# A transformer block in split fp32 on one core: the odd blocks' squares pass DRAM unrounded and are split on arrival, row stores go to ScalarE's queue, and some loads are issued at other places

## The chip, the cores and the metric

The kernel runs on one core of a Trainium2 chip. The metric is the device time of one execution in microseconds. The kernel before took 1139.48 us, the median of three runs (1138.54 to 1140.03).

## The reference, cut to what matters

```python
# S = 2048 rows, D = 576, 32 heads of Dh = 18, F = 4608, all fp32
def _A_ref(x, wqkv, wo):
    q, k, v = heads(x @ wqkv)
    W, dil = 8, 2                                     # each row sees itself and 7 rows, 2 apart
    idx = pos[:, None] - (arange(W) * dil)[None, :]
    logits = einsum("bhsd,bhswd->bhsw", q, k[idx]) * Dh ** -0.5
    attn = softmax(where(idx >= 0, logits, -1e9))
    return einsum("bhsw,bhswd->bhsd", attn, v[idx]) @ wo

def _B_ref(x, w1, b1, w2, b2):
    r = relu(x @ w1 + b1)
    return (r * r) @ w2 + b2

xn = layernorm(x)
out = x + _A_ref(xn, wqkv, wo) + _B_ref(xn, w1, b1, w2, b2)
```

## The kernel before, in words

**Split operands.** Every fp32 operand of a product is split in two: a rounded part `hi`, copied by ScalarE, and the rest `lo`, subtracted by VectorE (the helper `tt`, L94). A product is three matmuls: hi by hi, hi by lo, lo by hi.

**Blocks and stages.** The 2048 rows are four blocks b of 512 (TB), taken in two pairs s: (0, 1) and (2, 3). The stages follow each other on TensorE:

- the opening: x of block 0 is normalized row by row and turned, and the first of four head groups g gets its Q, K and V;
- `q0()` (L1072): the 28 other quarter-block rows of Q, K, V of blocks 0 and 1, 14 matmuls each;
- `phase_a(0)` (L634): the FFN of blocks 0 and 1 in 18 pairs p of 128-wide slices of F. `ffn_pair` (L505) forms both blocks' products x W1 together (L525, L529). Block 0's squares are multiplied with W2 at once (L494); block 1's go to DRAM. About 17.7 us a pair;
- block 0's attention output times wo, in five chunks c (`o_hi`, `o_lo`, `o_ops`);
- `phase_b0` (L759): block 1's squares come back from DRAM and are multiplied with W2, tile by tile (n = 0 to 35); between them the Q, K, V rows of blocks 2 and 3; then block 1 times wo;
- `phase_a(1)`, block 2 times wo, `phase_b1` (L835) and the tail: the same for blocks 2 and 3.

**The odd block's squares.** In `ffn_pair`, r0 and r1 are the two blocks' relu sums, in buffers `r4` (four of them, also used for u, for parts of Wqkv, for a part of the regrouped attention output and for o). In `finish_pair` (L545) ScalarE makes `h1`'s rounded square of r1 (L536) and the full square (L540), VectorE subtracts (L94, `h<-r,h`), and SP stores hi and lo, 1024 KB, in `hscr`. `load_h` (L755) brings both back into one of three `h` buffers, three pairs ahead.

**Q, K, V rows.** `qkv_out` (L294): ScalarE copies a row's sums into one of four slots j of the one buffer `st` (L295), and every second row three DMAs on SP store two slots in DRAM. A slot is written again four rows later, so the copy waits for the landing of that store. Five TensorE banks hold rows that are not yet copied. `split_wq` splits the next head group's weights on ScalarE (L261) and VectorE.

**Attention.** For each block and group, `attention(b, g)` (L343) is 18 pieces on VectorE; `side(k)` hands out k of them at places fixed in the code. Its q, k and v come from DRAM by `fetch()` in the order of `offer()`; they are issued on `lane[0]`, which is SP at first and POOL from row 6 of `q0` on. At the end of an attention eight stores on POOL (L382) write its output, and `release()` lets the next loads go. POOL works its queue in order: the stores, the q, k and v loads, and `regroup` (L683, L689), which reads a block's whole attention output (part 0 into `st`, part 1 into an `r4`). `o_hi` (L693) transposes that on VectorE (L700).

**Weights.** `load_w2` (L452, L457) keeps three raw tiles `w2r` and three split ones `w2s`; `w2_hi` and `w2_lo` split two tiles ahead. `load_w1` (L428) brings W1 of a pair in two 640 KB loads. Both are issued on SP, in program order with everything else there.

Of the kernel before, what the change touches and what calls it, by code (L numbers as in the profile page):

```python
# [8 lines left out]
F32 = mybir.dt.float32  # L9
# [7 lines left out]
P = 128  # L17
S, D, F = 2048, 576, 4608
H, DH, W, DIL = 32, 18, 8, 2
TB = 512  # L20
# [25 lines left out]
def block_kernel(ctx: ExitStack, tc: tile.TileContext, x, xt, wqkv, wo, w1, b1, w2, b2, out):  # L46
# [30 lines left out]
    b1t = const.tile([P, NF], F32, name="b1t")  # L77
    b2t = const.tile([P, 64], F32, name="b2t")[:, :NC]

    scr = {k: [dram.tile([PAD + S, CG], F32, name=f"{k}scr{g}") for g in range(G)] for k in "kvq"}  # L80
    OPART = ((0, OA), (OA, CG))
    oscr = {(b, k): dram.tile([P, NJ * G, z - a], F32, name=f"o{b}{k}") for b in range(NB) for k, (a, z) in enumerate(OPART)}
    mrscr = {b: dram.tile([2 * NJ, P], F32, name=f"mr{b}") for b in range(1, NB)}
    hscr = [[dram.tile([P, 4 * TB], F32, name=f"h{s}{p}") for p in range(NP)] for s in range(2)]

    def flat(t, off, parts, n):
        a = t[0:1, 0:1]
# [206 lines left out]
    def qkv_out(b, g, j, p):  # L294
        nc.scalar.activation(stage[0][:, j], p[:, :QW], AF.Copy)  # L295
        if j % 2:
            for i, k in enumerate("kvq"):
                nc.sync.dma_start(scr[k][g][PAD + b * TB:PAD + (b + 1) * TB].rearrange("(p j) c -> p j c", j=NJ)[:, j - 1:j + 1],
                                  stage[0][:, j - 1:j + 1, i * CG:(i + 1) * CG])

    def qkv_row(b, g, j, i):
        p = bank(i)
# [6 lines left out]
        a = t[:, j:j + 1, 0:1]  # L309
        return bass.AP(tensor=a.tensor, offset=a.offset, ap=[a.ap[0], [DIL * CG, W], *dims])  # L310

    loads, landed, queue, free, lane = [], {}, [], [0], [nc.sync]

    def fetch():
        while free[0] and loads:
            free[0] -= 1
            kind, b, g = loads.pop(0)
            if kind == "x":
                load_rows(b)
                landed["x", b] = True  # L320
                continue
            t = landed[kind, b, g] = sb.tile([P, NE, CG], F32, name="kv", bufs=3)
            if kind == "k":
                q = landed["q", b, g] = sb.tile([P, NJ, CG], F32, name="q", bufs=2)
                lane[0].dma_start(q.rearrange("p j c -> p (j c)"),
                                  flat(scr["q"][g], (PAD + b * TB) * CG, [NJ * CG, P], NJ * CG))
            lane[0].dma_start(t.rearrange("p e c -> p (e c)"),
                              flat(scr[kind][g], (PAD + b * TB - HALO) * CG, [NJ * CG, P], NE * CG))
# [176 lines left out]
    def ffn_pair(s, p, work, first=False):  # L505
# [38 lines left out]

        def finish_pair():  # L545
            r0, r1, h0 = prev.pop("r")
            h1 = square_hi(r1)
            square_lo(r0, h0)
            square(r1)
            yield  # L550
            square_lo(r1, h1)
            nc.sync.dma_start(hscr[s][p], h1.rearrange("p k f t -> p (k f t)").bitcast(F32))
            yield

        before = prev.pop("finish", None)
# [7 lines left out]
        if not last:  # L563
            combine_w1(n + 1)
        if not first:
            side(1 + p % 2, False)
        work(0)
        product(bb, T2, ss(2))
        w2_hi()
# [64 lines left out]
    def phase_a(s, filler):  # L634
        b = 2 * s
        ffn_pair(s, 0, filler, first=True)
        open_y(b)
        for p in range(1, NP):
            h, ops = hs.pop(s * NP + p - 1), []

            def work(i):
                if i in (0, 2):
                    ops.extend(tile_products(b, 2 * p - 2 + i // 2, h))
                add(b, ops[7 * i:7 * i + 7])

            if p == NP - 1:
                complete(b)
                regroup(b, 0)
                residual(b)
                if s == 0:  # L650
                    load_xt(2)
                    load_mb(2)
            ffn_pair(s, p, work)
        h, end = hs.pop(s * NP + NP - 1), prev.pop("finish")
        load_h(s, 0)
        next(end)
        regroup(b, 1)
        o_hi(b, 0), o_hi(b, 1)
        o_lo(b, 0), o_lo(b, 1)
        add(b, tile_products(b, NF - 2, h))  # L660
        w2_hi()
        w2_lo()
        next(end)
        load_h(s, 1)
        residual_left(b)
        o_hi(b, 2), o_hi(b, 3)
        o_lo(b, 2), o_lo(b, 3)
        add(b, tile_products(b, NF - 1, h))
        w2_hi()
        w2_lo()  # L670
        o_hi(b, 4)
        o_lo(b, 4)
        for c in range(NC):
            w2_hi()
            add(b, o_ops(b, c), range(NC) if c == NC - 1 else ())
            w2_lo()
            if c == 1:
                load_h(s, 2)
        finish(b)

    ob = {}
# [72 lines left out]

    def load_h(s, p):  # L755
        t = hs[s, p] = mt.tile([P, 2, 2, TB], F32R, name="h", bufs=3)
        nc.sync.dma_start(t.rearrange("p k f t -> p (k f t)").bitcast(F32), hscr[s][p])

    def phase_b0():  # L759
        b, r = 1, 0  # L760
        todo = [(2 + i, g, j) for g in range(G) for i in range(2) for j in range(NJ)]
        split_up.clear()
        open_stage()
        load_xt(3)
        load_wq(0)
        pieces = [normalize(2), once(load_mb, 3), split_wq(0, "S", lambda: load_wq(1)), normalize(3)]
        open_y(b)
        for n in range(NF):
            w2_hi()
            add(b, tile_products(b, n, hs[0, n // 2]))  # L770
            w2_lo()
            if n % 2 and n // 2 + 3 < NP:
                load_h(0, n // 2 + 3)
            run(pieces, 2 if n < 9 else 1)
            while r < 32 and 32 * (n - 6) > 22 * r:
                bb, g, j = todo[r]
                while bb not in normed or g not in split_up:
                    run(pieces, 1)
                qkv_row(bb, g, j, 2 + r % 3)
                r += 1  # L780
                if r == 2:
                    pieces.append(split_wq(1, "w1s", lambda: load_wq(2)))
                if r == 8:
                    pieces.append(split_wq(2, "S", lambda: load_wq(3)))
                if r == 16:
                    pieces.append(split_wq(3, "w1s"))
                if r == 24:
                    pieces.append(sums(1))
                if j == NJ - 1 and bb == 2:
                    offer(2, g)  # L790
                run(pieces, 2)
            if n == 28:
                run_all(pieces)
                last_sum(1)
                complete(1)
                load_w1(NP)
                load_w1(NP + 1)
                regroup(b, 0)
                regroup(b, 1)
                for g in range(G):  # L800
                    offer(3, g)
            if n == 33:
                residual(b)
                combine_w1(NP)
            if n in (33, 34):
                c = 2 * (n - 33)
                o_hi(b, c), o_hi(b, c + 1)
                o_lo(b, c), o_lo(b, c + 1)
        o_hi(b, 4)
        o_lo(b, 4)  # L810
        residual_left(b)
        for c in range(3):
            w2_hi()
            add(b, o_ops(b, c))
            w2_lo()
            if c == 1:
                w1_hi(NP, 0)
                w1_lo(NP, 0)

        def filler(i):  # L820
            if i < 2:
                add(b, o_ops(b, 3 + i), range(NC) if i else ())
            if i == 0:
                w1_hi(NP, 1)
                w1_lo(NP, 1)
            if i == 1:
                finish(b)

        return filler
# [5 lines left out]
    def phase_b1():  # L835
        b = 3
        open_y(b)
        for n in range(NF - 2):
            w2_hi()
            add(b, tile_products(b, n, hs[1, n // 2]))  # L840
            w2_lo()
            if n % 2 and n // 2 + 3 < NP:
                load_h(1, n // 2 + 3)
            if b not in xr and (n == 22 or not queue and current[0] is None):
                complete(b)
                regroup(b, 0)
                regroup(b, 1)
                residual(b)
                residual_left(b)
            if n in range(27, 27 + NC):  # L850
                o_hi(b, n - 27)
                o_lo(b, n - 27)
            side(2)
        for c in range(NC):
            w2_hi()
            add(b, o_ops(b, c), (NC - 2,) if c == NC - 1 else ())
# [215 lines left out]
    def q0():  # L1072
        todo = [(b, g, j) for b, g in ((0, 1), (0, 3), (0, 2), (1, 3), (1, 2), (1, 1), (1, 0)) for j in range(NJ)]
        pieces = [statistics(1), split_wq(3, "S")]

        held = []

        def row(r):
            b, g, j = todo[r]
# [3 lines left out]
            if j == NJ - 1:  # L1083
# [2 lines left out]
                    if not b and g > 1:  # L1086
                        offer({3: 2, 2: 3}[g])

                if r < 2:
                    held.append(go)  # L1090
                else:
                    go()

        for r in range(len(todo) - 2):
            row(r)
            if r == 1:
                run(pieces, 1)
                turn_mr(1, 7)
                load_mb(1)
            if r == 2:  # L1100
                run_all(pieces)
                load_wq(2)
                offer(0, 0)
                for late in held:
                    late()
                held.clear()
                pieces += [normalize(1)]
            if r == 6:
                lane[0] = nc.gpsimd
                load_w1(0)  # L1110
                pieces.insert(0, split_wq(2, "h", lambda: load_wq(0)))
            if r == 11:
                run_all(pieces)
            if r == 15:
# [91 lines left out]
```

## Time and profile before

| | before |
|---|---|
| median of three runs | 1139.48 us |
| profiled execution | 1139.25 us |
| its span | 1137.5 us |
| granted TensorE clock, mean | 0.998 |
| DMA, mean over the span | 224 GB/s |

In the views quoted below, a row of a timeline is start and length in us, engine, line, operation, output and inputs, count, and in brackets the idle time ahead of it with what ended it. A row of a group is count, busy us, mean ns, and the idle us ahead. A row of the waits is the total idle us, the number of waits, and the longest. A row of a window is its length, then the busy us (and instructions) of TensorE, its weight loads, VectorE, ScalarE and POOL, then the granted clock, the DMA engines' share and GB/s. A row of DMA issues is count, KB each and the median us from issue to landing. A row of the chain is start, length and what the time was spent on.

### The profile page before, as it was taken

The numbers are of one execution on the slowest core, as the hardware profiler recorded it, in microseconds if no ns is written. First come the engines' busy times: TensorE is split into PE (matmuls) and PEld (weight loads), VectorE is DVE, ScalarE is ACT, GpSimd is POOL, SyncE is SP. The second block draws the span as 40 slices with busy tenths as digits, with TensorE's granted clock in tenths as the row PEclk, the third lists the DMA queues.
The fourth block names the chain that finished last, engine by engine and source line by source line (L and its number), as shares of the span: only waits on it lengthen the run. The fifth ranks groups of instructions, "written<-read, shape, count | busy, mean of one in ns | idle before, by whom it ended". The sixth has DMA issues, their size and how long they took to land.

```text
span 1137.5 us, 13818 instructions
## 1 busy us (share of the span) xinstructions
PE 1117.7 (98%) x5014; PEld 937.1 (82%) x5014; DVE 912.6 (80%) x1202; ACT 575.1 (51%) x801; POOL 115.1 (10%) x219
## 2 busy tenths in 40 slices
PE   8899999999999999999999899999999999999998
PEld 6799788888888887889998777888888888887787
DVE  7696999899988966888777779789897978789453
ACT  5334767666666663422222256766667666422131
POOL 4001001020200100022101001001020100101100
PEclk9999999999999999999999999999999999999999
DMA  7857544576575679887785944645464562887982
GB/s 278 293 178 221 183 167 165 194 188 218 185 204 189 212 270 327 331 306 241 252 275 168 346 160 158 234 139 191 173 234 161 181 240 100 290 305 256 343 296 88
DMA packets 89477, 254.26 MB, mean 224 GB/s; under 512 B 12472, under 2 KB 40896, under 8 KB 74816
## 3 DMA queue, kind: packets, MB, share of 16 engines
q1 hardware_dynamic: 78576, 200.86, 50.9%
q0 software_dynamic: 10544, 52.14, 14.0%
q8 instruction: 39, 0.64, 0.2%
q10 hardware_dynamic: 288, 0.37, 0.1%
q14 instruction: 30, 0.25, 0.1%
HBM read 191.90 MB, written 61.43 MB: 223 GB/s over the span
## 4 chain that ended last, share of the span: by engine, by line
PE 83%; DVE 7%; DMA 5%; issue 2%; ACT 1%; SPq 1%; POOL 1%; ACTq 0%; DVEq 0%; POOLq 0%
PE p L494 35%; PE p L525 29%; PE p L305 13%; PE p L529 5%; DMA w2r<-in_w 2%; DVE w2s L94 2%; DVE pr L94 1%; PE p L989 1%; DMA h<-h 1%; DMA qscr<-st 1%; DVE w1s L94 1%; DVE lg L354 1%; DMA q<-qscr 1%; DVE w1r L94 0%; DVE h L94 0%
## 5 line engine op out<-in xcount | busy, mean ns | idle before, releaser
L494 PE MATMUL p<-h,w2s 128*128 128x512 f32 x2010 | 486.4, 390 | 3.4 <-DMA h<-h 1.4
L494 PEld LDWEIGHTS p<-h,w2s 128*128 128x128 f32 x2010 | 376.2, 188 | 86.4 <-ACT w2s L467 2.7
L525 PE MATMUL p<-X,w1s 128*128 128x512 f32 x864 | 219.5, 389 | 1.6 <-DVE r L94 1.6
L525 PEld LDWEIGHTS p<-X,w1s 128*128 128x128 f32 x864 | 162.0, 188 | 36.0 <-DVE r L94 2.4
L94 DVE TENSOR_TENSOR w2s<-w2r,w2s 128x576 fp32r<-128x576 f32 x164 | 123.4, 755 | 84.0 <-ACT w2s L467 83.5
L467 ACT ACTIVATE w2s<-w2r 128x640 fp32r<-128x640 f32 x164 | 119.6, 733 | 119.1 <-DMA w2r<-in_w 63.6
L525 PE MATMUL p<-S,w1s 128*128 128x512 f32 x648 | 164.6, 389 | 0.0
L525 PEld LDWEIGHTS p<-S,w1s 128*128 128x128 f32 x648 | 121.5, 188 | 25.5 <-DVE r L94 0.3
L382 POOL DMA_DIRECT2D o<-q x128 | 69.4, 607 | 620.2 <-DVE q L94 618.2
L94 DVE TENSOR_TENSOR h<-r,h 128x1024 fp32r<-128x1024 f32 (+2 forms) x78 | 93.1, 1198 | 42.5 <-ACT r L540 35.4
L295 ACT ACTIVATE st<-p 128x432 f32<-128x432 f32 x64 | 33.6, 529 | 145.1 <-PE p L305 93.9
L94 DVE TENSOR_TENSOR w1s<-w1r,w1s 128x1024 fp32r<-128x1024 f32 x72 | 88.1, 1223 | 23.4 <-ACT w1s L440 23.3
L532 ACT ACTIVATE r<-r,b1t 128x512 f32<-128x512 f32 x72 | 52.0, 722 | 108.4 <-DVE r L94 108.4
L94 DVE TENSOR_TENSOR pr<-q,kv 128x1152 f32<-128x1152 f32 x64 | 86.8, 1356 | 1.3
L94 DVE TENSOR_TENSOR pr<-lg,kv 128x1152 f32<-128x1152 f32 x64 | 86.7, 1355 | 1.2
L354 DVE TENSOR_REDUCE lg<-pr 128x64 f32<-128x1152 f32 x64 | 86.4, 1350 | 0.9
L94 DVE TENSOR_TENSOR pr<-pr 128x576 f32<-128x576 f32 (+1 forms) x128 | 77.7, 607 | 3.5
L440 ACT ACTIVATE w1s<-w1r 128x1024 fp32r<-128x1024 f32 x72 | 75.7, 1052 | 4.0 <-PE p L494 4.0
L536 ACT ACTIVATE h<-r 128x1024 fp32r<-128x1024 f32 x72 | 76.0, 1056 | 1.1
L540 ACT ACTIVATE r<-r 128x1024 f32<-128x1024 f32 x72 | 76.0, 1055 | 1.2
L529 PE MATMUL p<-x,w1s 128*128 128x512 f32 x216 | 66.5, 389 | 0.0
L494 PE MATMUL p<-w1s,w2s 128*128 128x512 f32 x260 | 61.0, 391 | 3.5 <-ACT w2s L467 3.3
(135 smaller groups left out, 1043.8 us busy)
## 6 DMA issues: line engine op xcount, KB each, us to landing
h<-h SPq DMA_DIRECT2D x72, 1024.0 KB, 5.5
w2r<-in_w SPq DMA_DIRECT2D x144, 320.0 KB, 4.7
w1r<-in_w SPq DMA_DIRECT2D x36, 640.0 KB, 4.8
kv<-vscr POOLq DMA_DIRECT2D x15, 1296.0 KB, 8.0
kv<-kscr POOLq DMA_DIRECT2D x14, 1296.0 KB, 8.2
r<-in_wqkv SPq DMA_DIRECT2D x16, 432.0 KB, 5.9
w2r<-in_wo SPq DMA_DIRECT2D x20, 320.0 KB, 4.8
w1r<-in_xt SPq DMA_DIRECT2D x6, 1024.0 KB, 7.5
```

The source lines that it names most:

```text
L94: return nc.vector.tensor_tensor(out=out, in0=a, in1=b, op=op)
L305: nc.tensor.matmul(p[:, :QW], l, r, start=k == 0, stop=k == len(mm) - 1)
L354: nc.vector.tensor_reduce(out=lg[:, j * HG:(j + 1) * HG].rearrange("p a w -> p w a"), in_=pr.rearrange("p w (a d) -> p w a d", d=DH), axis ...
L382: nc.gpsimd.dma_start(rows[:, i], q[i * L:(i + 1) * L, :, a:z])
L440: nc.scalar.activation(w1s[n, k][:, 0], raw1[n][:, 4 * k:4 * k + 4], AF.Copy)
L467: nc.scalar.activation(w2s[stream[i]][:, :DE], raw2[i], AF.Copy)
L494: nc.tensor.matmul(yp[b][c], v, a, start=c not in yb[b], stop=c in last and c not in [o[0] for o in ops[i + 1:]], skip_group_check=True)
L525: nc.tensor.matmul(to, l, r, start=start and i == 0, stop=i == len(mm) - 1, skip_group_check=True)
L529: nc.tensor.matmul(to, weight(LEFT, k, f), v, start=False, stop=k == 1, skip_group_check=True)
L532: nc.scalar.activation(to, a, AF.Relu, bias=b1t[:, f:f + 1])
L536: nc.scalar.activation(h[:, 0], r, AF.Square)
L540: nc.scalar.activation(r, r, AF.Square)
```

## The change

Six parts:

1. `hscr` is half as large. `finish_pair` squares r1 in place (L540) and stores that, unrounded; the square `h1` and its subtraction are gone. `load_h` loads 512 KB into the `lo` half of the tile; the new `h_hi` copies it rounded into the `hi` half on ScalarE, and `h_lo` subtracts in place on VectorE. They are called for pair 0 in the wo part of `phase_a`, and for the next pair at every second tile of `phase_b0` and `phase_b1`.
2. The Q, K, V rows are stored by ScalarE's queue; the three scratches of a group are parts of one DRAM tile.
3. In `q0`, block 1's statistics are turned and loaded (`turn_mr`, `load_mb`) after row 2 rather than row 1; the first attentions' loads are offered after row 6, on POOL, rather than after row 2, on SP; `load_w1(0)` moves from row 6 to row 10.
4. In phase A, `side()` at the start of a pair gives 2 + p % 2 pieces in pair pass 0 (it was 1 + p % 2) and 1 + p % 2 in pass 1 (as before); for p = 1 it gives 1 (it was 2).
5. In `phase_b0`, `load_w1(NP)` moves from tile 28 to tile 20; at tile 28 the regroups are issued ahead of the attention's next loads, and `load_w1(NP + 1)` behind those.
6. In `phase_b1`, `side(2)` becomes `side(1 + n % 2)`.

```diff
-    scr = {k: [dram.tile([PAD + S, CG], F32, name=f"{k}scr{g}") for g in range(G)] for k in "kvq"}
+    kvq = [dram.tile([3, PAD + S, CG], F32, name=f"kvq{g}") for g in range(G)]
+    scr = {k: [kvq[g][i] for g in range(G)] for i, k in enumerate("kvq")}
...
-    hscr = [[dram.tile([P, 4 * TB], F32, name=f"h{s}{p}") for p in range(NP)] for s in range(2)]
+    hscr = [[dram.tile([P, 2 * TB], F32, name=f"h{s}{p}") for p in range(NP)] for s in range(2)]
...
-                nc.sync.dma_start(scr[k][g][PAD + b * TB:PAD + (b + 1) * TB].rearrange("(p j) c -> p j c", j=NJ)[:, j - 1:j + 1],
-                                  stage[0][:, j - 1:j + 1, i * CG:(i + 1) * CG])
+                nc.scalar.dma_start(scr[k][g][PAD + b * TB:PAD + (b + 1) * TB].rearrange("(p j) c -> p j c", j=NJ)[:, j - 1:j + 1],
+                                    stage[0][:, j - 1:j + 1, i * CG:(i + 1) * CG])
...
     def fetch():
-        while free[0] and loads:
+        while free[0] and loads and not held[0]:
...
         def finish_pair():
             r0, r1, h0 = prev.pop("r")
-            h1 = square_hi(r1)
             square_lo(r0, h0)
             square(r1)
             yield
-            square_lo(r1, h1)
-            nc.sync.dma_start(hscr[s][p], h1.rearrange("p k f t -> p (k f t)").bitcast(F32))
+            nc.sync.dma_start(hscr[s][p], r1.rearrange("p f t -> p (f t)"))
             yield
...
         if not first:
-            side(1 + p % 2, False)
+            side(1 if p == 1 else (2 if s == 0 else 1) + p % 2, False)
...
         for c in range(NC):
             w2_hi()
+            if c == 2:
+                h_hi(s, 0)
             add(b, o_ops(b, c), range(NC) if c == NC - 1 else ())
             w2_lo()
             if c == 1:
                 load_h(s, 2)
+            if c == 2:
+                h_lo(s, 0)
...
-        nc.sync.dma_start(t.rearrange("p k f t -> p (k f t)").bitcast(F32), hscr[s][p])
+        nc.sync.dma_start(t[:, 1].rearrange("p f t -> p (f t)").bitcast(F32), hscr[s][p])
+
+    def h_hi(s, p):
+        if p < NP:
+            t = hs[s, p]
+            nc.scalar.activation(t[:, 0], t[:, 1].bitcast(F32), AF.Copy)
+
+    def h_lo(s, p):
+        if p < NP:
+            t = hs[s, p]
+            tt(t[:, 1], t[:, 1].bitcast(F32), t[:, 0].bitcast(F32), ALU.subtract)
...
         for n in range(NF):
             w2_hi()
+            if n % 2 == 0:
+                h_hi(0, n // 2 + 1)
             add(b, tile_products(b, n, hs[0, n // 2]))
             w2_lo()
+            if n % 2 == 0:
+                h_lo(0, n // 2 + 1)
...
+            if n == 20:
+                load_w1(NP)
             if n == 28:
                 run_all(pieces)
                 last_sum(1)
+                held[0] = True
                 complete(1)
-                load_w1(NP)
-                load_w1(NP + 1)
                 regroup(b, 0)
                 regroup(b, 1)
+                held[0] = False
+                fetch()
+                load_w1(NP + 1)
...
-            side(2)
+            side(1 + n % 2)
...
-                if r < 2:
-                    held.append(go)
+                if r < 6:
+                    waiting.append(go)
...
-            if r == 1:
-                run(pieces, 1)
+            if r == 2:
                 turn_mr(1, 7)
                 load_mb(1)
-            if r == 2:
                 run_all(pieces)
                 load_wq(2)
-                offer(0, 0)
-                for late in held:
-                    late()
-                held.clear()
                 pieces += [normalize(1)]
             if r == 6:
                 lane[0] = nc.gpsimd
+                offer(0, 0)
+                for late in waiting:
+                    late()
+                waiting.clear()
+                pieces.insert(0, split_wq(2, "h", lambda: load_wq(0)))
+            if r == 10:
                 load_w1(0)
-                pieces.insert(0, split_wq(2, "h", lambda: load_wq(0)))
```

More of the change, by code (lines that the diff above doesn't have):

```diff
@@ L310, in shifted @@
         return bass.AP(tensor=a.tensor, offset=a.offset, ap=[a.ap[0], [DIL * CG, W], *dims])
-    loads, landed, queue, free, lane = [], {}, [], [0], [nc.sync]
+    loads, landed, queue, free, lane, held = [], {}, [], [0], [nc.sync], [False]
     def fetch():
-        while free[0] and loads:
+        while free[0] and loads and not held[0]:
             free[0] -= 1
@@ L839, in phase_b1 @@
             w2_hi()
+            if n % 2 == 0:
+                h_hi(1, n // 2 + 1)
             add(b, tile_products(b, n, hs[1, n // 2]))
             w2_lo()
+            if n % 2 == 0:
+                h_lo(1, n // 2 + 1)
             if n % 2 and n // 2 + 3 < NP:
@@ L1074, in q0 @@
         pieces = [statistics(1), split_wq(3, "S")]
-        held = []
+        waiting = []
         def row(r):
```

## The prediction

> **What bounds the kernel now.** I read three views: the busy shares and the chain of waits on the page, then what TensorE's idle time waited for, then timelines around each wait.
>
> ```profile
> PE 1117.7 (98%) x5014; PEld 937.1 (82%) x5014; DVE 912.6 (80%) x1202; ACT 575.1 (51%) x801; POOL 115.1 (10%) x219
> ...
> PE 83%; DVE 7%; DMA 5%; issue 2%; ACT 1%; SPq 1%; POOL 1%; ACTq 0%; DVEq 0%; POOLq 0%
> ```
> ```profile
> PE p L494 <- ACT w2s L467: 4.7, 5, 2.2
> PE p L305 <- ACT h L261: 4.3, 1, 4.3
> ...
> PE p L525 <- DVE r L94: 1.6, 2, 0.9
> PE p L494 <- DMA h<-h: 1.4, 1, 1.4
> PE p L163 <- POOL mr L130: 1.0, 1, 1.0
> ```
>
> TensorE is busy 98% of the span. No matmul is added or removed, so a gain can come only out of its idle time, and behind the start-up this list holds nearly all of it: 4.7 + 4.3 + 1.6 + 1.4 + 1.0 = 13.0 us in ten places. (Some cost a little more, since the clock falls behind them.) A loss has no such ceiling: whatever makes TensorE wait in a new place is added whole. So I go through the ten waits, and then look for an eleventh.
>
> **The opening.** The longest single wait:
>
> ```profile
> 44.39 0.55 PE L305 MATMUL p<-S,x 128*128 128x432 f32 x2
> 49.28 4.29 PE L305 MATMUL p<-h,X 128*128 128x432 f32 x12 [4.34 <-ACT h L261]
> ...
> 53.80 2.50 PE L305 MATMUL p<-h,X 128*128 128x432 f32 x12
> ...
> 56.54 2.50 PE L305 MATMUL p<-h,X 128*128 128x432 f32 x12
> ```
> ```profile
> 28.22 0.29 PE p L163
> ...
> 39.34 0.37 SPq L298
> ...
> 40.27 7.14 DMA qscr<-st
> ```
>
> The 12 matmuls behind the gap take 4.29 us, where the same 12 take 2.50 later: a gap of this length costs 1.8 us beyond itself. The chain says why it opens. ScalarE must copy the next row's sums into `st`, whose slot is free only when the stores issued from 39.34 have landed, 7.14 us after the last issue; the split of the weights (L261) stands behind that copy. The change acts on it from both sides.
> - For: the 1.0 us wait of L163 goes, since the statistics are turned a row later. The q, k and v loads that crowd the stores leave SP for POOL, where nothing is ahead of them, so they start and end earlier, and the stores could land in 2 to 4 us rather than 7.
> - Against: a row takes 56.54 - 53.80 = 2.74 us, so L163 moves from 28.22 to about 28.22 - 1.0 + 2.74 = 30.0, and with it the normalized block, on which ScalarE waits ahead of its copies. ScalarE now issues the stores itself, three per pair of rows at about 0.37 us and a little more each: 1.2 us at the least.
>
> With landings as long as now, TensorE resumes about 1.8 + 1.2 = 3.0 us later than at 49.28; with landings 3 to 5 us shorter, between then and 2 us earlier. I take 0.3 us gained, between -3 and +2. Later in this stage the same stores delay nothing as long as TensorE's five banks hold the rows that ScalarE has not copied.
>
> The Trainium skill (DMA: Bandwidth & Descriptors, Issuing engines are not separate DMA queues) speaks against part of this: transfers started by any engine share the same 16 DMA engines, and a second issuing engine saves only its issue time. By that rule alone the landings would stay at 7.14 us, the opening would lose 3.0 us, and the forecast would be 3.3 us later; that loads start earlier is not covered by it, and no run here shows it yet.
>
> **Phase A's steady part.** Two of the ten waits are in pairs 1 and 19, for VectorE's sum `r` (1.6 us in all). Each pair loses the subtraction `h<-r,h` of the odd block; in phase A(0) one more piece of attention is put in its place; and pairs 1 and 19 lose a piece besides.
>
> ```profile
> L94 DVE TENSOR_TENSOR h<-r,h 128x1024 fp32r<-128x1024 f32 x32 | 39.1, 1222 | 15.0 <-ACT r L540 15.0
> L94 DVE TENSOR_TENSOR pr<-q,kv 128x1152 f32<-128x1152 f32 x18 | 24.4, 1356 | 0.3
> ```
> ```profile
> 130.00:418.00 288.00, 287.36 (x1268) 237.59 (x1268) 253.51 (x344) 188.10 (x247) 30.06 (x55) 1.00 0.63 207
> ```
>
> Pairs 1 and 19 become 1.22 + 1.36 = 2.6 us lighter, more than the longest wait there (0.9): both waits go, 1.6 us gained. In the other pairs of A(0) the exchange is -1.22 + 1.36 = +0.14 us, hidden behind VectorE's idle 288 - 254 = 34 us over 16 pairs, about 2 us a pair. I take nothing; without that cover it would be 16 x 0.14 = 2.2 us. ScalarE's 36 fewer squares only make it freer here.
>
> **The end of phase A(0): the eleventh wait.** Some 16 more pieces in A(0) are nearly an attention (18 pieces), so attentions end at other places. In the order of the changed kernel's instructions, attention (1,2) ends in pair 17: its last `q` on VectorE stands behind the pair's sum r0. Behind it on POOL's queue come its eight stores, the next q load (which waits until all eight have landed), a k load, and only then the regroup r<-o of block 0, which TensorE needs for the wo products. In before this regroup was long through:
>
> ```profile
> 416.12 0.69 DVE L94 TENSOR_TENSOR r<-p,r 128x512 f32<-128x512 f32 x1 [0.95 <-PE p L529]
> 416.73 1.35 DVE L94 TENSOR_TENSOR pr<-lg,kv 128x1152 f32<-128x1152 f32 x1
> ...
> 426.43 0.67 DVE L700 STREAM_TRANSPOSE r<-r 128x512 f32<-128x512 f32 x1
> ```
> ```profile
> 425.99 14.90 PE L494 MATMUL p<-w1s,w2s 128*128 128x512 f32 x65
> ```
> ```profile
> DMA  9999999999996779100000189999999999896799
> ...
> r<-o POOLq DMA_DIRECT2D x1, 384.0 KB, 6.8
> ```
>
> (The first line is the DMA engines' busy share, in tenths, in 40 slices of 1.125 us from 400 on; the second has the microseconds from issue to landing.)
>
> Exactly this sequence is in the trace already, at the end of phase A(1), where it has room:
>
> ```profile
> 963.33 1.25 DVE L94 TENSOR_TENSOR pr<-pr 128x576 f32<-128x576 f32 x2
> 964.61 0.31 DVE L94 TENSOR_TENSOR q<-pr 128x144 f32<-128x144 f32 x1
> ```
> ```profile
> 965.21 1.64 POOL L382 DMA_DIRECT2D o<-q  x3 [42.67 <-DVE q L94]
> 967.23 2.69 POOL L382 DMA_DIRECT2D o<-q  x5 [0.38 <-issue]
> 975.04 0.56 POOL L325 DMA_DIRECT2D q<-qscr  x1 [5.12 <-DMA o<-q]
> 975.59 0.56 POOL L327 DMA_DIRECT2D kv<-kscr  x1
> 976.12 0.56 POOL L689 DMA_DIRECT2D r<-o  x1
> ```
> ```profile
> r<-o POOLq DMA_DIRECT2D x1, 384.0 KB, 9.0
> ```
>
> Worked out for A(0): r0's sum is bound by TensorE, so the next work starts at 416.73; pr, pr and q take 964.92 - 963.33 = 1.59 us: q ends at 418.3. From there by the A(1) rows: 976.12 - 964.92 = 11.2 us to the regroup's issue and 9.0 to its landing, so 438.5. The short end: the issues take 969.92 - 964.92 = 5.0, the stores land in 1.9 (row below), q and k loads are issued in 1.1, the regroup lands in 6.8: 433.1. VectorE then transposes and splits (0.67), subtracts and, behind that, finishes wo's second chunk. The same steps stand in these rows from 650.05 to 652.81, 2.8 us:
>
> ```profile
> 650.05 0.67 DVE L700 STREAM_TRANSPOSE r<-r 128x512 f32<-128x512 f32 x1
> ...
> 652.05 0.76 DVE L94 TENSOR_TENSOR w2s<-w2r,w2s 128x576 fp32r<-128x576 f32 x1
> ```
>
> So the chunk is there at 435.9 to 441.3. TensorE wants it at its 20th wo matmul (14 of the first chunk, 5 of the second): 425.99 + 19 x 14.90/65 = 430.3. The new wait is 5.6 to 11.0 us. I take 9.0, nearer the A(1) rows, because SP's loads of w2 and h fall into the same stretch. A wait of this length brings the slow matmuls too, 1.8 us as above: 10.8 in all. Nothing hides it: all wo chunks and the next phase are behind it on TensorE, and `w2_lo` of later chunks is behind it on VectorE. In A(1) attention (3,0) ends at the same instruction as before, so that end stays.
>
> **Phase B0 and its end.** h_hi (ScalarE) and h_lo (VectorE, 1.22 us as above) come 18 times, 22 us of VectorE over 200 us in which it was idle for 43:
>
> ```profile
> 445.00:645.00 200.00, 199.31 (x936) 175.31 (x934) 157.00 (x187) 57.89 (x91) 25.05 (x46) 1.00 0.79 276
> ```
>
> That fits, since w2 is split two tiles ahead; without the cover, 18 x 1.22 = 22 us. At its end TensorE waits for w2 loads that queue behind larger ones:
>
> ```profile
> 647.51 3.49 PE L494 MATMUL p<-w1s,w2s 128*128 128x512 f32 x14 [2.23 <-ACT w2s L467]
> 652.07 4.75 PE L494 MATMUL p<-w1s,w2s 128*128 128x512 f32 x18 [1.07 <-ACT w2s L467]
> ```
> ```profile
> DMA packets 2844, 8.12 MB, mean 325 GB/s; under 512 B 384, under 2 KB 1216, under 8 KB 2557
> ...
> w1r<-in_w SPq DMA_DIRECT2D x2, 640.0 KB, 5.4
> h<-h SPq DMA_DIRECT2D x1, 1024.0 KB, 9.9
> ...
> o<-q POOLq DMA_DIRECT2D x4, 48.0 KB, 1.9
> ```
>
> One of the two W1 loads goes eight tiles earlier, and h is halved: 640 + 512 KB = 1.18 MB less in this stretch (620 to 645), at 325 GB/s 3.6 us. The two waits are 3.3 us; I take 3.3 (bounds 1.5 and 4). The other two w2 waits near 454 and 458 (4.7 - 2.23 - 1.07 - 0.70 = 0.7) stand behind the same h loads: 0.7 gained, bounds 0 and 1.
>
> **Phase B1.** There remain 0.70 us for w2 and 1.4 for an h load. Half the bytes and half the side pieces speak for both going; h_hi and h_lo now stand between landing and use. I take 1.3, between 0 and 2.1.
>
> **Sum.** Gains 0.3 + 1.6 + 0.7 + 3.3 + 1.3 = 7.2; loss 10.8; net +3.6. The profiled execution took 1139.25 us (span 1137.5), 0.23 under the median of the three runs, so 1139.25 + 3.6 = 1142.8, and with the bounds 1137 to 1148.
>
> **Rivals.**
> 1. *The regroup's lateness is cheap and the gains are whole* (faster). The row of digits shows the DMA engines idle from 419 to 425, just when the eight stores would go. With the short end the wait is 5.6, and if the earlier loads also shorten the opening by 2 and all waits behind it go (13.0 - 4.3 - 1.0 = 7.7), the sum is 1139.25 - 9.7 + 5.6 = 1135; if the stores, too, overlap more than in A(1) and the wait is halved, 1132. Against it: it needs every bound at its good end.
> 2. *ScalarE is held by its own stores* (slower). Its 96 issues have waits of their own, for earlier DMAs; if landings stay at 7 us, each pair of rows in the opening is behind the last, TensorE's gap at 44 grows, so that it resumes 3.0 late, a second one of the kind follows where it now has none (4.3 + 1.8), and the wait at 430 stays: 1142.8 + 3.3 + 6.1 = 1152. It decides as soon as the copy into `st` comes later than TensorE's fifth bank. Against: the list of waits has only one of this kind.
> 3. *The halved transfers were hidden anyway.* h has three buffers; if the waits at 645 and in B1 stay, 3.3 + 1.3 are not gained: 1147.
>
> **How the numbers follow.** Forecast 0.57, rival 1 0.30, rival 2 0.05, rival 3 0.08. A difference under 0.2% (2.3 us) can't be told from none here. The forecast's own spread (1139 to 1147) gives 0.39 slower, 0.17 same, 0.01 faster; rival 1 0.29 faster, 0.01 same; the others slower: 0.30 faster, 0.18 same, 0.52 slower. The range 1132.5 to 1147.5 takes in rival 1 nearly whole and leaves out rival 2.
>
> **What would show it.** A wait of TensorE near 430 for w2s, with r<-o landing at 433 to 439: right. No wait there, or r<-o ahead of the stores on POOL: the main step is wrong. Waits near 130 and 689 gone; the ones at 645 and 650 under 1 us; the gap at 44 between 2 and 6 us. A time under 1137 would make the forecast wrong, as would new waits spread through phase A(0).

## The result and the profile after

The changed kernel took 1158.95 us (median of four runs, 1156.48 to 1159.96), the kernel before 1139.76 beside it: a ratio of 1.0166, 95% interval 1.0147 to 1.0185. It is slower by 19 us. The forecast, 1142.8, had the sign and its main cause, and was far too small; the time lies outside its range of 1132.5 to 1147.5.

First the busy shares of the page, then what TensorE's idle time waited for, in the changed kernel:

```profile
PE 1123.4 (97%) x5014; PEld 942.1 (81%) x5014; DVE 913.8 (79%) x1202; ACT 572.3 (49%) x801; POOL 120.3 (10%) x224
```
```profile
PE p L495 <- ACT w2s L468: 14.4, 4, 10.5
PE p L306 <- ACT h L262: 7.7, 1, 7.7
PE p L495 <- ACT h L765: 2.4, 1, 2.4
...
PE p L1014 <- ACT X L99: 0.9, 1, 0.9
PE p L526 <- DVE w1s L95: 0.5, 1, 0.5
```

TensorE runs the same 5014 matmuls in both kernels and is busy 5.7 us longer (1123.4 against 1117.7): some run slower, besides the waits. Since the matmuls come in the same order, the time at which the same one starts in both traces says where the 20.2 us between the spans (1157.7 - 1137.5) arise:

| stage, up to the matmul at (before) | starts later by | this stage |
|---|---|---|
| opening and q0, 120.3 | 7.5 | +7.5 |
| pair 1, 131.1 | 6.7 | -0.8 |
| end of A(0): wait 10.5, then slow matmuls, 432.1 | 19.9 | +13.2 |
| start of B0: wait 2.4, then slow matmuls, 458.0 | 23.0 | +3.1 |
| end of B0, 655.6 | 21.0 | -2.0 |
| pair 19, 690.3 | 20.0 | -1.1 |
| end of A(1): wait 2.1, then slow matmuls, 991.3 | 23.8 | +3.8 |
| B1, 1074.3 | 19.9 | -3.9 |

The last matmul is 20.1 later. Four rows of TensorE's timeline stand for the four losses, each with its wait in brackets and what followed it:

```profile
53.17 5.06 PE L306 MATMUL p<-h,X 128*128 128x432 f32 x12 [7.65 <-ACT h L262]
...
446.32 5.91 PE L495 MATMUL p<-w1s,w2s 128*128 128x512 f32 x13 [10.50 <-ACT w2s L468]
...
476.25 6.10 PE L495 MATMUL p<-h,w2s 128*128 128x512 f32 x19 [2.37 <-ACT h L765]
...
1010.51 11.66 PE L495 MATMUL p<-w1s,w2s 128*128 128x512 f32 x43 [2.14 <-ACT w2s L468]
```

At the pace of before's wo products (65 in 14.90 us), the 13 matmuls of the second row would take 3.0 us. They take 5.9, at a granted clock of 0.50: of the 13.2 us, 10.5 are the wait and 2.7 the slow matmuls behind it.

The chain of waits of the changed kernel at the end of A(0) (start, length, what):

```profile
424.54 0.32 DVE q L95
...
425.15 3.26 POOL o L383 x6
...
429.07 2.34 DMA o<-q
...
432.17 0.45 POOL q L326
...
433.28 10.96 DMA r<-o
...
446.32 12.54 PE p L495 x42
```

This is the forecast's eleventh wait, link by link: the last q, the stores on POOL, their landing, the q and k loads, and only then the regroup.

### The profile page after: what moved, and what is told of

Read it like the earlier page. It is cut to its first block, busy times and chain, and to the rows that moved or that the text cites. A ratio compares the mean times of both kernels' runs of the same rounds, so it can differ in the third digit from the quotient of the medians.

```text
span 1157.7 us, 13855 instructions
## 1 busy us (share of the span) xinstructions
PE 1123.4 (97%) x5014; PEld 942.1 (81%) x5014; DVE 913.8 (79%) x1202; ACT 572.3 (49%) x801; POOL 120.3 (10%) x224
## 4 chain that ended last, share of the span: by engine, by line
PE 85%; DVE 5%; DMA 5%; ACT 2%; issue 1%; ACTq 1%; POOL 0%; SPq 0%; POOLq 0%; DVEq 0%
PE p L495 40%; PE p L526 28%; PE p L306 11%; PE p L530 5%; DVE pr L95 1%; DMA r<-o 1%; PE p L1014 1%; DVE w1s L95 1%; ACTq L299 1%; DVE w1r L95 1%; DVE w2s L95 1%; DMA h<-h 1%; DMA r<-in_wqkv 1%; DMA mr<-mrt 0%; DVE r L95 0%
## 5 line engine op out<-in xcount | busy, mean ns | idle before, releaser
L95 DVE TENSOR_TENSOR h<-r,h 128x1024 fp32r<-128x1024 f32 (+2 forms) x42 | 49.2, 1180 | 40.8 <-ACT r L541 35.1
L495 PE MATMUL p<-w1s,w2s 128*128 128x512 f32 x260 | 65.7, 411 | 14.6 <-ACT w2s L468 14.4
L495 PEld LDWEIGHTS p<-w1s,w2s 128*128 128x128 f32 x260 | 51.5, 200 | 27.9 <-ACT w2s L468 16.1
```

The lines of the kernel that those rows point to most:

```text
L95: return nc.vector.tensor_tensor(out=out, in0=a, in1=b, op=op)
L495: nc.tensor.matmul(yp[b][c], v, a, start=c not in yb[b], stop=c in last and c not in [o[0] for o in ops[i + 1:]], skip_group_check=True)
```

## The experiments

The kernel before ran beside each group of runs: 1140.32 us beside 1 to 4 below (`pieces`, `regroup_sp`, `q0_undone`, `rows_sp`), 1139.71 beside `q0_rows_undone`, `hstore_act`, `combo` and `combo_hfirst`, 1139.08 beside `combo_spread`, `combo_no5` and `part1_only`, 1138.85 beside `loads_sp`. Where no interval stands, it is a single run.

**1. `pieces`: fewer pieces in A(0).**

```diff
-            side(1 if p == 1 else (2 if s == 0 else 1) + p % 2, False)
+            side(1 if p == 1 else 1 + p % 2, False)
```

> The changed kernel with phase A(0)'s 16 additional pieces taken back. Theory (the regroup r<-o waits on POOL behind the stores and loads of an attention that ends in pair 17): TensorE's wait of 10.5 us at 435 falls to about 2, what the landing of the last h<-r store alone would leave, as at the end of A(1) (2.1); with the slow matmuls behind it the time falls by 8 to 12, to about 1149. Rival (the r4 buffer that the last r1 keeps until its store has landed is the cause at both ends): the wait stays above 5 and the time falls by less than 5.

1147.99 us. TensorE's and VectorE's timelines of this run:

```profile
437.80 7.41 PE L495 MATMUL p<-w1s,w2s 128*128 128x512 f32 x25 [2.31 <-ACT w2s L468]
```
```profile
435.75 0.71 DVE L703 STREAM_TRANSPOSE r<-r 128x512 f32<-128x512 f32 x1 [4.17 <-DMA h<-r]
```

The wait falls from 10.5 to 2.3, and behind it stands another one: VectorE's transposition writes into an `r4` buffer, and the one that is next held the last r1 until its store h<-r has landed. Before the change VectorE's subtraction was the last to read r1, and no store did. Both causes are real; the regroup hid the second. From 131.1 to 432.1 of the table this run loses 3.9 us, where the changed kernel loses 13.2.

**2. `regroup_sp`: the regroups on SP's queue.**

```diff
-        nc.gpsimd.dma_start(t.rearrange("p r c -> p (r c)"), oscr[b, k]...)
+        nc.sync.dma_start(t.rearrange("p r c -> p (r c)"), oscr[b, k]...)
```

> The changed kernel with all regroups issued on SP instead of POOL, and nothing else. Theory (POOL's order is what makes the regroup late): r<-o is issued before the attention's stores have landed, the wait at 435 falls to 2 to 4, and the time falls by 7 to 12, to about 1149. Rival (the transfers themselves are slow in this stretch, whatever the queue): r<-o still lands after 440 and the wait stays above 7.

1161.27 us. The wait at 435 fell to 2.4, as expected, so POOL's order is the cause there. But SP works in order too, and a regroup on it waits with the h loads behind it: near 645 for 11.5 us, by the profile for the last store of the rows out of `st`, into which it reads, and near 1100 for 4.4 us for an attention's stores. This run's waits and timeline of TensorE:

```profile
PE p L495 <- ACT h L765: 10.8, 3, 4.7
```
```profile
655.41 4.76 PE L495 MATMUL p<-h,w2s 128*128 128x512 f32 x11 [4.66 <-ACT h L765]
```

The waits for h grow from 2.4 to 10.8 in all, near 650 and in B1, which gives the gain back.

**3 to 6. The opening.** Part 3 alone taken back (`q0_undone`), part 2 alone (`rows_sp`), both (`q0_rows_undone`), and part 3 kept with the first attentions' loads on SP (`loads_sp`):

```diff
 # loads_sp
             if r == 6:
-                lane[0] = nc.gpsimd
                 offer(0, 0)
                 for late in waiting:
                     late()
                 waiting.clear()
+                lane[0] = nc.gpsimd
```

> The changed kernel with part 3 taken back: statistics turned after row 1, first attention loads on SP after row 2, load_w1(0) at row 6; row stores stay on ScalarE. Theory (the q, k and v loads that POOL issues from 29.9 crowd the store and the load of the statistics, 5.3 and 3.6 us): the gap at 45 falls from 7.7 to about 5 and the time by 3 to 5, to about 1155. Rival (ScalarE is held by its own store issues): the gap stays above 7 and the time within 1.5.

> The changed kernel with part 2 taken back: Q, K, V rows stored by SP again, part 3 kept. Theory (the loads crowd the statistics): the gap at 45 stays at 6 to 8, the time falls by 1 to 3 through the 1.1 us wait near 19 and the short ones near 106 to 127, to about 1157. Rival (ScalarE's store issues hold it): the gap falls to about 4.5 and the time by 4 to 6.

> The changed kernel with parts 2 and 3 both taken back. Theory (the two together make the opening's loss, the rows by ScalarE's issues near 19 and 106 to 127, the q0 order by the crowded statistics): the gap at 45 is 4.3 again, the waits near 19 and 106 to 127 are gone, and TensorE passes 130 at the same time as in before, 6 to 7 us earlier than in the changed kernel; time about 1151 to 1152. Rival (the loads of part 1 or 5 or the merged scratch tile also cost there): 2 or more of those 6 to 7 us stay.

> The changed kernel with the first two attentions' loads issued on SP at the same place of the code, behind the load of the statistics, instead of on POOL. Theory (the opening's gap grew because POOL issues 2.9 MB of q, k and v from 29.9 on, ahead of the store and the load of the statistics at 33.4 and 38.7): the store lands in about 2 us instead of 5.3, block 1 is normalized about 3 us earlier than at 42.3, and the gap at 45 falls from 7.7 to 4 to 6; time about 1154 to 1156, the other waits as they were. Rival (the row stores on ScalarE and the turn one row later delay it, the loads do not): the normalization still begins after 41 and the gap stays above 7.

They took 1154.42, 1153.46, 1148.22 and 1156.36 us. In the same order, each one's row for the gap in TensorE's waits (7.7 in the changed kernel):

```profile
PE p L306 <- ACT h L262: 5.3, 1, 5.3
```
```profile
PE p L306 <- ACT h L262: 9.8, 1, 9.8
```
```profile
PE p L306 <- ACT h L262: 4.3, 1, 4.3
```
```profile
PE p L306 <- ACT h L262: 7.0, 1, 7.0
```

With both parts undone, TensorE is within 0.6 us of the kernel before until 429: the opening's loss is parts 2 and 3, and nothing of parts 1 and 5. The gap alone is a coarse measure, since in the four kernels that share this opening (the changed one, `pieces`, `regroup_sp`, `hstore_act`) it is 7.7 to 9.4 us long. Steadier is how late TensorE is at the table's first matmul, 120.3: 7.2 to 7.9 us in these four, 5.7 with part 2 alone, 4.7 with part 3 alone, 6.4 in `loads_sp`, and 0.2 to 1.5 in the six kernels with neither. So either part alone costs most of what both cost together. Part 3 makes the gap long, with SP's stores (9.8) as with ScalarE's (7.7 to 9.4). Part 2 adds only 1.0 to the gap (5.3 against 4.3), but it spreads the rest: its three store issues take ScalarE 1.43 us each time, and with the rows back on SP the waits near 19 and 106 to 127 are gone, and TensorE is 2.8 us earlier at 120.3 in spite of the gap.

`rows_sp` and `q0_rows_undone` came out about 3 us lower than was expected. Some 2 us of that lie outside the opening: their waits at the end of A(0) (10.6 and 10.4) and at the start of B0 (2.4 and 2.4) are as long as the changed kernel's, but fewer slow matmuls follow them. The last section shows when they do.

How part 3 does it stands in the changed kernel's chain and POOL's timeline:

```profile
33.37 5.27 DMA mr<-mrt
...
38.69 3.57 DMA mb<-mr
...
42.29 1.24 DVE w1r L95
```
```profile
29.87 0.62 POOL L326 DMA_DIRECT2D q<-kvq  x1
30.55 1.10 POOL L328 DMA_DIRECT2D kv<-kvq  x2
```

The store of the statistics, 4 KB, takes 5.27 us, and POOL has put 2.9 MB of q, k and v ahead of it. In `loads_sp`, where they are issued behind it, it takes 1.22 us, and the normalization begins 3.4 us earlier, as expected of the crowding (the chain, then VectorE's timeline):

```profile
33.20 1.22 DMA mr<-mrt
```
```profile
38.91 4.88 DVE L95 TENSOR_TENSOR w1r<-w1r,mb 128x1024 f32<-128x1024 f32 x4 [4.54 <-DMA mb<-mr]
```

But the gap hardly shrinks, 7.0 where 4 to 6 was expected: now the loads are on their way when the rows' stores are issued, and ScalarE's copy waits for the landing of those, 6.99 us after the last issue, as in the kernel before (7.14). In these two orders the same bytes hit one of the two chains or the other.

**7. `hstore_act`: the last link of A(0) and A(1).**

```diff
-            nc.sync.dma_start(hscr[s][p], r1.rearrange("p f t -> p (f t)"))
+            nc.scalar.dma_start(hscr[s][p], r1.rearrange("p f t -> p (f t)"))
```

> The changed kernel with the store of r1 issued by ScalarE right behind the square, instead of by SP. Theory (a transposition at the end of phase A waits until the last r1's buffer r4 is free, which is when its store has landed, and SP issues that store late, behind a w2 load): the 2.1 us wait at 1008 goes, and the time falls by 2 to 4, to about 1156; the 10.5 us wait at 435 stays, since the regroup is later still. Rival (the transposition there waits for the regroup): the wait at 1008 stays.

1150.57 us. VectorE's transposition at the end of A(1), in the changed kernel and in this run:

```profile
1008.46 0.71 DVE L703 STREAM_TRANSPOSE r<-r 128x512 f32<-128x512 f32 x1 [4.03 <-DMA h<-r]
```
```profile
1000.01 0.71 DVE L703 STREAM_TRANSPOSE r<-r 128x512 f32<-128x512 f32 x1
```

The wait is gone, and with it TensorE's. The time fell by 8.4, more than twice what was expected: by the matched matmuls 4.0 us at the end of A(1), 3.2 at the end of A(0), where the regroup landed in 8.66 us instead of 10.96 and TensorE waited 8.5, and 1.0 at the start of B0, where the wait is as long as before and fewer slow matmuls follow. That the store, issued earlier, was out of the regroup's way is likely, and not shown:

```profile
433.94 8.66 DMA r<-o
```

**8. `combo`: parts 2, 3 and A(0)'s pieces taken back, r1's store on ScalarE; parts 1, 5 and 6 kept.** Of part 4 the one piece less in pairs 1 and 19 is kept too.

> Parts 2, 3 and A(0)'s additional pieces taken back, and the store of r1 on ScalarE; part 1 (unrounded squares), part 5 and part 6 stay. Theory: no wait at 45 beyond 4.4, none at 435 and 1000, and the gains of before's waits at 130, 645, 689, 1042 and 1072 stay; the wait for h near 460 (2.3) stays: 1136 to 1139, faster than before by 1 to 4. Rival (the split on arrival costs more than the other parts give): 1140 or more.

1135.27 us (five runs, 1134.83 to 1137.23), ratio to the kernel before 0.9964, interval 0.995 to 0.9978: 0.4% faster than the kernel before, and clear of the noise. Its waits of TensorE:

```profile
PE p L306 <- ACT h L262: 4.3, 1, 4.3
PE p L495 <- ACT h L765: 2.4, 1, 2.4
...
PE p L495 <- ACT w2s L468: 1.6, 2, 1.1
```

**9 and 10. The wait for h at the start of B0.** `combo_hfirst` puts h_hi ahead of w2_hi in both B phases; `combo_spread` changes this line of `phase_b0` in `combo`:

```diff
-            run(pieces, 2 if n < 9 else 1)
+            run(pieces, 1 if n in (1, 2) else 2 if n < 9 else 1)
```

> The run before this one with the rounded copy of h (h_hi) ahead of the w2 copy on ScalarE in both B phases, not behind it. Theory (near 460 the copy of h is queued on ScalarE behind a w2 copy and behind a normalized block that VectorE delivers late): the wait for h there goes, 1.5 to 2.5 us less than the run before. Rival (VectorE is what is late, so any order of ScalarE waits for it): the wait turns into one for w2s of the same size, no difference.

> The run 'combo' with one piece instead of two of the normalization behind tiles 1 and 2 of phase B0. Theory (from 444 on VectorE and ScalarE wait for each other in a round of 4.9 us a tile, normalize, X, w2 copy, w2 subtraction, against TensorE's 3.2 us, and the split of h is put on top): with two pieces fewer in the round the wait of 2.4 us at 453 falls to under 0.8, and the time by 2 to 3, slow matmuls included, to about 1133. Rival (the pieces only move the wait back to a later tile, because block 2's first Q, K, V row needs them): the same wait at 456 to 465, no difference.

`combo_hfirst` took 1138.12 us (ratio 0.9991, interval 0.998 to 1.0002): the same 2.4 us became a wait for w2s, as the rival said. But it is 2.9 us slower than `combo`, which neither said: in its profiled run block 1's regroup is issued 1.6 us later than in `combo` and lands in 12.26 us instead of 10.73, and at 648 TensorE waits 3.3 us, where `combo` waits 0.6 and 1.1. Whether the order on ScalarE brought that is open. `combo_spread` took 1152.05 us (1.0114, 1.0097 to 1.013). The round of VectorE and ScalarE, in `combo`'s timelines of the two:

```profile
449.59 0.76 DVE L95 TENSOR_TENSOR w2s<-w2r,w2s 128x576 fp32r<-128x576 f32 x1 [1.75 <-ACT w2s L468]
450.27 2.48 DVE L95 TENSOR_TENSOR w1r<-w1r,mb 128x1024 f32<-128x1024 f32 x2
454.50 0.76 DVE L95 TENSOR_TENSOR w2s<-w2r,w2s 128x576 fp32r<-128x576 f32 x1 [1.75 <-ACT w2s L468]
```
```profile
452.78 1.06 ACT L181 ACTIVATE X<-w1r 128x1024 fp32r<-128x1024 f32 x1 [3.22 <-DVE w1r L95]
453.75 0.72 ACT L468 ACTIVATE w2s<-w2r 128x640 fp32r<-128x640 f32 x1
454.37 1.04 ACT L765 ACTIVATE h<-h 128x1024 fp32r<-128x1024 f32 x1
```

ScalarE waits for VectorE's normalization, VectorE for ScalarE's w2 copy: 4.9 us a round. In `combo_spread` the place was right (there TensorE is 1.1 us ahead of before at 454, where `combo` is 1.3 behind), with 0.85 us of wait at 460. But at 648 it waits 3.2 us and has lost that again, and in B1 the attention work ran out of step: a run of attention pieces from 1080.44 to 1092.40 fills VectorE, with w2's split behind them, and TensorE waited 10.8 us at 1082 (the waits of TensorE, then VectorE's timeline at the end of it):

```profile
PE p L495 <- DVE w2s L95: 11.0, 2, 10.8
```
```profile
1080.44 1.36 DVE L95 TENSOR_TENSOR pr<-lg,kv 128x1152 f32<-128x1152 f32 x1
...
1092.40 1.42 DVE L95 TENSOR_TENSOR w2s<-w2r,w2s 128x576 fp32r<-128x576 f32 x2
```

**11 and 12. Parts 5 and 1 alone.** `combo_no5` is `combo` with part 5 taken back; `part1_only` is the kernel before with part 1 (and the merged scratch tile).

> The run 'combo' with part 5 taken back (both W1 loads at tile 28 ahead of the regroups, no hold). If the earlier W1 load is what made the w2 loads near 640 earlier, the waits at 647 and 651 grow from 1.6 to about 2.8 to 3.5 and the time by 1.5 to 2; if halving h did it, they stay within 0.5.

> The kernel before with part 1 alone (and the three scratches of a group as one tile): squares through DRAM unrounded, stored by SP, split on arrival; phase B1 with its two pieces per tile. Theory: waits of 2.3 at about 429 and 987 (the transposition waits for the last r1's store) and 2.4 near 453 (the split of h), about 9 with the slow matmuls behind them; gains of 0.8 and 0 to 1 at 130 and 689 and of 1 to 3.5 in B1: 1141 to 1144. Rival (halving the transfers pays for all of it): under 1139.

`combo_no5` took 1135.23 us, against 1135.27 with part 5, and from 458.0 to 655.6 of the table it gains 1.6 us, against 1.8: moving W1's load bought next to nothing. `part1_only` took 1153.15, slower than its own theory. The three waits were there (2.36, 2.35 and 2.36 us at 429, 456 and 990), but B1 lost where a gain was expected: from 997 to 1074 (before's 990 to 1058) TensorE fell back by 9.2 us more. B1 in 60 us, in `part1_only` and then in the changed kernel (length, busy us of TensorE, its weight loads, VectorE, ScalarE, POOL):

```profile
1015.00:1075.00 60.00, 51.98 (x215) 38.76 (x214) 56.28 (x74) 20.26 (x26) 4.89 (x10) 1.00 0.51 167
```
```profile
1030.00:1090.00 60.00, 60.00 (x265) 49.43 (x264) 56.84 (x73) 24.03 (x31) 4.88 (x9) 1.00 0.62 205
```

VectorE is nearly full in both, and only the second does not make TensorE wait. `combo_no5`, which differs from `part1_only` only in part 6, in the queue of r1's store and in one piece of pairs 1 and 19, gains 4.0 us in B1: part 1 needs part 6's fewer pieces there.

## Why the prediction was right and wrong

- **The end of A(0): right, undersized.** The chain is the forecast's, and `pieces` and `regroup_sp` show it. Predicted were 9.0 us of wait (5.6 to 11.0) and 1.8 of slow matmuls; measured 10.5 and about 2.7. The regroup landed in 10.96 us, beyond the long end of 9.0 that the sum used.
- **The opening: wrong in sign.** The step that failed is "leave SP for POOL, where nothing is ahead of them, so they start and end earlier". They did start earlier, and so came ahead of the statistics' store and load, on which the normalization waits. I let the normalized block come later only by the row that the turn was moved (1.8 us), with its store and load as short as before, and took 0.3 us gained, between -3 and +2; the stage lost 7.5: TensorE resumed 3.9 us late (53.17 against 49.28), more slow matmuls cost 1.4, and the waits from 106 to 127 cost 2.2. The rows' stores did land sooner, in 3.9 us in the middle from 20 to 60, which did not help, since the normalized block ahead of the copies on ScalarE was late. `q0_rows_undone` shows that parts 2 and 3 hold all of it. The rule of the Trainium skill that I weighed and set aside (DMA: Bandwidth & Descriptors, Issuing engines are not separate DMA queues) fits better than my choice: transfers issued from any engine interleave on the same 16 engines. By it I had reckoned 3.0 us lost, still too little: here loads from POOL held up SP's 4 KB (5.27 us, against 1.22 in `loads_sp`).
- **"Later in this stage the same stores delay nothing": wrong.** On ScalarE the row stores cost 2.8 us at 120.3 on top of part 3; with part 2 alone TensorE is 5.7 us late there, against 0.2 to 1.5 with neither part.
- **"So that end stays" at A(1): wrong.** The attention did end at the same instruction. What I left out is that r1, once stored itself, keeps its buffer until the store has landed; `hstore_act` shows it. It cost 3.8 us.
- **"That fits" in B0: wrong at its start.** 22 us of VectorE against 43 idle is an average over 200 us; the first tiles have no slack (a round of 4.9 us against TensorE's 3.2), and the stage there lost 3.1 us, where I had counted 0.7 gained.
- **Pairs 1 and 19: right.** 0.8 and 1.1 gained, 1.9 against 1.6. `part1_only`, which keeps the piece that part 4 takes out there, gains the same: the subtraction that is gone is enough.
- **End of B0 and B1: right sign, wrong sizes and one wrong reason.** 2.0 against 3.3, and 3.9 against 1.3. `combo_no5` shows that the earlier W1 load, which my sum counted, gave next to nothing. That halving h gave what was gained at the end of B0 fits `part1_only` (waits of 1.1 and 1.1 there, against 2.2 and 1.1), which has it without part 5.

Of the rivals, the slower one that ScalarE is held by its own stores was true in a smaller form: waits near 19 and 106 to 127 rather than a second long gap, and 5.7 us late by part 2 alone where it reckoned 9.1 (3.0 + 4.3 + 1.8).

## What to carry to other kernels

Before work is moved into a stage, list what ends where in the new order: work on an in-order queue holds whatever is issued behind it, and here one attention that ended at the wrong place cost 9.3 us (13.2 with it, 3.9 in `pieces`), more than all the stages that gained (0.8 + 2.0 + 1.1 + 3.9 = 7.8). A buffer that is now the source of a DMA is free only when that has landed, so look for the next writer of it. And an idle share over a stage says nothing about its first few microseconds, where several pieces of work start together.

## What I had not expected of the hardware

A short wait can slow the matmuls behind it as much as the 4.34 us one of the opening did (1.8 us), and does so only sometimes. Behind 2.14 us of wait at 1010 the changed kernel's 43 matmuls took 11.66 us, 1.8 more than at before's pace of 14.90/65; behind 2.36 us in `combo` 13 took 4.84, 1.9 more; behind 2.23 us at 647 in before, 14 took 3.49, only 0.3 more:

```profile
455.46 4.84 PE L495 MATMUL p<-h,w2s 128*128 128x512 f32 x13 [2.36 <-ACT h L765]
```

The granted clock in the traces shows what makes the difference. It changes only at the edges of steps of 3.41 us, which lie fixed in time through a run, whatever the kernel does: in the changed kernel, stretches at 0.50 begin at 438.47, 476.01 and 1011.91, 11 and 157 steps apart. The same wait of 2.36 us at the start of B0, cut into such steps, in `combo` and then in `hstore_act`:

```profile
452.32:455.73 3.41, 1.05 (x5) 0.59 (x4) 1.47 (x3) 2.63 (x3) 0.00 (x0) 1.00 1.04 406
455.73:459.14 3.41, 3.41 (x9) 2.64 (x9) 3.37 (x4) 1.11 (x2) 0.00 (x0) 0.50 0.41 129
```
```profile
468.12:471.53 3.41, 2.79 (x13) 1.97 (x11) 2.40 (x3) 0.94 (x1) 0.00 (x0) 1.00 1.04 411
471.53:474.94 3.41, 1.67 (x7) 1.41 (x8) 2.45 (x3) 1.69 (x3) 0.00 (x0) 1.00 0.90 318
474.94:478.35 3.41, 3.00 (x13) 2.15 (x13) 3.18 (x5) 2.51 (x4) 0.00 (x0) 1.00 0.13 51
```

In `combo` the wait lies whole in one step (3.41 - 1.05 = 2.36 us idle), and the next runs at 0.50, which costs half of it, 1.7 us. In `hstore_act` an edge cuts the wait into 0.62 and 1.74 us, and the clock stays at 1.00. In the 14 traces of this case, from 25 us on, the clock fell behind each of the 35 full-speed steps with 1.98 us of idle TensorE or more, and behind none with 1.85 us or less.

The Trainium skill (TensorE: Matmul & The Clock Gate, Why this matters for your kernels) names idle gaps of more than about 3 us; these are shorter, and the measurement decides. Where the edges fall against the waits differs from run to run, so a difference of 1 to 2 us between single runs can be this alone: of the 8.4 us by which `hstore_act` fell, the 1.0 at the start of B0 is.
